# A fused attention and spectral-mixing kernel: a fixed order of weight loads, x times w_ch moved behind the attention, and two spreads held back until the last weights have landed

## The chip, the core and the metric

The kernel runs on one core of a Trainium2 chip. The metric is the device time of one execution in microseconds (us). Three timed runs of the kernel before gave 440.73, 440.25 and 440.62 us; their median is 440.62. The profiled execution took 440.91 us as a whole, and its span, from the first to the last instruction that the profile shows, is 439.1 us.

Engines are named as in the profile: PE multiplies matrices (PEld loads its stationary operand), DVE and ACT are the vector and scalar engines, POOL issues the large loads from DRAM, SP issues the small transfers and the output.

## What is computed

Attention over 8 batches and 8 heads (576 positions, head size 64) with a causal mask and a decay bias, and then, on its output x (8 x 576 x 512), a mixing in the frequency domain and a residual block:

```python
scores = scale * q @ k.T ; scores = where(causal, -1e9, scores + minimum(-(cum_i - cum_j), 0))
x = softmax(scores) @ v                      # heads side by side: 8 x 576 x 512
X = rfft(x, axis=1)                          # only the first 64 modes are used
Yr = einsum('bmd,mde->bme', Xr, w_r) - einsum('bmd,mde->bme', Xi, w_i)
Yi = einsum('bmd,mde->bme', Xr, w_i) + einsum('bmd,mde->bme', Xi, w_r)
y = irfft(Yr + 1j * Yi, n=576, axis=1)       # zero beyond mode 64
u = x + y
out = u + maximum(u @ w_ch, 0)
```

w_r and w_i are 64 x 512 x 512 each in float32: 134 MB that are read once. Everything else is small beside them.

## The kernel before

**Groups, chunks, tiles.** The 512 columns of x are cut into 4 groups of 128 (two heads each), the 64 modes into 8 chunks of 8. A weight tile is one group, one chunk, and one of w_r and w_i: 64 tiles, numbered 0 to 63 in the order of use, each 1 MB on chip (bf16), loaded by two DMAs of 512 KB. Chunk product c (0 to 31, `modes`, L470) uses tiles 2c and 2c+1: sixteen matmuls, the first eight on the w_r tile, the other eight on the w_i tile. Groups 0 to 2 (chunks 0 to 23) add into `y_acc`; group 3 (chunks 24 to 31) adds the last part and gives the spectrum `yb` of its chunk.

**The first four tiles** lie in memory that is free early (`early`, L199). The others rotate through two rings, five tiles (`wpool`) and three (`wpool2`); `ring_of` (L209) says which. From tile 38 on only the ring of five is used, because `wpool2` then takes kept products. A tile is loaded once the tile that had its place has been used.

**The attention loop** (L591) runs over n = 0 to 31, one group and one batch per step. POOL issues, in this order by step: q and k of a later step (every second step), v, and the weight tiles up to `on_chip[n]`. `on_chip` comes from a plan (L254 to L270): up to step 7 about one tile a step, then 1.5 tiles a step, then 2, cut back where a ring has no free place. `mode_steps` says which chunk products stand in which step: chunks 0 to 3 in step 8, then one or so per step, so that all of chunks 0 to 23 are inside the loop. The transformed x of a group (`fft`, L450) goes to one of two buffers, `xs[g % 2]`.

**x times w_ch.** The output needs (x + y) @ w_ch. y @ w_ch is made chunk by chunk (`y_times_wch`), x @ w_ch is made ahead for 18 pairs of row tiles; two pairs stay in PSUM, 16 are kept on chip (`kept`). For one pair x is transposed on PE (`x_transposed`, or `first_transposed` inside the loop), multiplied by w_ch (`x_times_wch`) and copied by ACT to its place (`keep`). Six of the 16 pairs (`first_pairs`, L527) are done inside the last six steps of the loop, one in the middle of chunk 30. The other nine are done by `work()`, called between the chunk products of group 3: `TAKE = (3, 2, 3, 0, 0, 0)` calls after chunks 24, 25 and 26, and two more inside `gather` of chunk 27 (its turns 1 and 3).

**Group 3.** After each product the chunk's spectrum is transposed (`y_transposed`). The first four chunks are then turned into rows of `yv`, by `gather(0, 4)` after chunk 27: four turns, each with two sets of eight matmuls (L729) and four copies by ACT and DVE in alternation (L739, L741) that follow each other. Chunks 28 and 29 go through `y_times_wch` (L710), a DMA (`spread`, L511) and a second `gather` of their own after chunk 29, which also has three transposes of x and x @ w_ch of pair 0. Chunks 30 and 31 are spread into `yv` by DMAs on SP: `spread(6, 0)` when the spectrum of chunk 30 is made, `spread(6, 1)` when its product with w_ch is made, and both again for chunk 31. Between the quarters of chunk 31 stand `first_z` and `first_u`, the sums for pairs 0 and 1 that use chunk 30 from SBUF (`add_last`) and rows below `GK` of `yv`, so not the rows of chunks 30 and 31.

**The end.** The list of steps from L955 on makes the 18 pairs of outputs in an order written by hand, and SP writes them out. The first step that reads all 128 rows of `yv` is U1.

Of the kernel before, what the change touches and what calls it, by code (L numbers as in the profile page):

```python
# [19 lines left out]
def kernel(  # L20
# [11 lines left out]
    nc = tc.nc  # L32
# [82 lines left out]
    auxpool = aux.enter_context(tc.tile_pool(name="aux_psum", bufs=2, space=PSUM, side="right"))  # L115

    dpool = ctx.enter_context(tc.tile_pool(name="dram", bufs=1, space=bass.MemoryType.DRAM))
    ncum_dram = dpool.tile([NPAIR, S + HP], BF16, name="ncum_dram")
    at = ExitStack()
    ap_ = at.enter_context(tc.tile_pool(name="attn", bufs=1))  # L120
# [125 lines left out]


    NW = 2
    mode_steps = {B: [0, 1, 2, 3], B + 1: [4], B + 2: [5], B + 4: [6], B + 6: [7]}
    for c in range(NCK, (NG - 1) * NCK):  # L250
        mode_steps.setdefault(B + c - (0 < c % NCK < 4), []).append(c)
    used = [NW * sum(len(cs) for t, cs in mode_steps.items() if t < n) for n in range(N + 1)]
    W0 = 2
    on_chip = []  # L254
    for n in range(N):
        w = 4 + 2 * (WA + WB + NE - 2) * (n + 1) // (B + 1) if n < B else plan + (3 if n <= 2 * B else 4)
        plan = w

        nt, ring = 0, ([], [])
        while nt < min(w // 2, len(wq)):  # L260
            i = ring_of(nt)
            if i is not None:
                depth = (WA, WB)[i]
                if len(ring[i]) >= depth and ring[i][-depth] >= used[n]:
                    break
                ring[i].append(nt)
            nt += 1
        if nt < w // 2:
            plan = 2 * nt + 1
        on_chip.append(2 * nt)  # L270


    nc.sync.dma_start(out=s_sb, in_=s.rearrange("b h t -> (b h) t"))
# [176 lines left out]
    def fft(n):  # L450
        if n < 0:
            return
        g, b = divmod(n, B)
        ps = auxpool.tile([P, 2, 3 * HM], FP32, name="ft_ps", tag="aux")
        for T in range(NT):
            nT = tails[T]
            for q_ in range(2):
                nc.tensor.matmul(  # L458
                    ps[HP * q_ : HP * q_ + HP].rearrange("p h f -> p (h f)"),
                    x_all[:nT, g, b, T, q_::2], Ff_sb[:nT, T, :],  # L460
                    start=(T == 0), stop=(T == NT - 1),
                    tile_position=(0, HP * q_), skip_group_check=True,
                )
        for h in range(2):
            for q_ in range(2):
                a = ps[HP * q_ : HP * q_ + HP, h, : 2 * HM].rearrange("p (r m) -> p r m", r=2)
                a = bass.AP(tensor=a.tensor, offset=a.offset, ap=[a.ap[0], [HM, 2]] + list(a.ap[1:]))
                nc.vector.tensor_copy(out=xs[g % 2][HP * h : HP * h + HP, q_, :, h, :, b, :], in_=a)  # L468

    def modes(g, c, meanwhile=None):  # L470


        ps = auxpool.tile([P, DM], FP32, name="yp", tag="aux")
        cols = xs[g % 2].rearrange("p q k h r b m -> p q k (h r b) m")

        def product(ri, q_, cg):
            k0 = HP if ri == 1 and c == 0 and cg == 0 else 0
            nc.tensor.matmul(  # L478
                ps[32 * cg : 32 * cg + 32, :],
                cols[k0:, q_, 1 - ri, :, c * MC // 2 + cg],  # L480
                wt[(g, c, ri)][cg // 2][k0:, 2 * (cg % 2) + q_, :],
                start=(ri == 0 and q_ == 0), stop=(ri == 1 and q_ == 1),
                tile_position=(k0, 32 * cg), skip_group_check=True,
            )

        for x in range(4):
            ri, y = divmod(x, 2)
            if meanwhile and x in meanwhile:
                meanwhile[x]()
            for z in range(4):  # L490
                if meanwhile:
                    product(ri, z // 2, 2 * y + z % 2)
                else:
                    product(ri, y, z)
        if g == 0:
            nc.vector.tensor_copy(out=y_acc[:, c, :], in_=ps)
# [27 lines left out]

    ways = dict(zip(kept, "vsgmsgsgmsgsgsgs"))

    first_pairs = [i for i in kept[1:] if pairs[i][0][1] < NF and pairs[i][0][0] <= 4][:6]  # L527
    z1s, xts1 = {}, {}

    def kept_place(i, t):  # L530

# [12 lines left out]
    def first_transposed(i, x):  # L544
        b, T = pairs[i][x]
        ps = auxpool.tile([P, DT, P], FP32, name="xt_ps", tag="aux")
        for dt in range(DT):
            nc.tensor.matmul(
                ps[:, dt, :], x_all[:, dt, b, T, :], ident16h, start=True, stop=True,
                skip_group_check=True,  # L550
            )
        xts1[i, x] = spool.tile([P, DT, P], FP16, name="xt1", tag="yt")
        nc.vector.tensor_copy(out=xts1[i, x], in_=ps)

    open_unit = {}

    def half_of(pool, name):
# [8 lines left out]
    def first_product(i, x):  # L566
        if x == 0:
            kept_place(i, half_of(wpool2, "z1"))
        ps = auxpool.tile([P, DM], FP32, name="z1_ps", tag="aux")
        for dt in range(DT):  # L570
            nc.tensor.matmul(
                ps, xts1[i, x][:, dt, :], wch_sb[:, dt, :], start=(dt == 0), stop=(dt == DT - 1)
            )
        keep_product(i, x, ps)


    def mode_products(n, half=None):
        cs = mode_steps.get(n, [])
# [3 lines left out]
    with tc.tile_pool(name="sc_psum", bufs=2, space=PSUM) as scpool, \  # L582
# [6 lines left out]
        load(loads_qk(2) + loads_v(2))  # L589
        pad_p()  # L590
        for n in range(N):  # L591
            if n in (0, 2):
# [17 lines left out]
            mode_products(n)  # L610
            transposes(n + 1, 0)
            scores(n, 1)
            i = first_pairs[n - N + len(first_pairs)] if n >= N - len(first_pairs) else None
# [8 lines left out]
            if i is not None:  # L622
                first_product(i, 1)
        av(N - 1, 1)
        fft(N - 1)
    load(loads_w(2 * len(wq)))
# [16 lines left out]
    NLOC = 5  # L643
    old = xs_flat[0]
# [6 lines left out]
    places = [finpool.tile([P, 4 * DM], BF16, name="r_sb", tag="r", bufs=3) for i in range(2)]  # L651
    places += [finpool.tile([P, 4 * DM], BF16, name=f"z1_{i}") for i in range(NLOC)]
    places.append(old[:, 4 * DM : 8 * DM])
# [33 lines left out]
    def keep(i):  # L687
        x_times_wch(i, True)
        j = late.index(i)
        kept_place(i, places[j])  # L690
        for x in range(2):
            keep_product(i, x, zs.pop((i, x)))

# [13 lines left out]
    def y_times_wch(c, yt):  # L707
        vp = auxpool.tile([P, DM], FP32, name="v_ps", tag="aux")
        for dt in range(DT):
            nc.tensor.matmul(  # L710
                vp, yt[:, dt, :], wch_sb[:, dt, :], start=(dt == 0), stop=(dt == DT - 1)
            )
# [171 lines left out]
    yb6 = modes(NG - 1, c, {2: lambda: keep(late[-1])})  # L884
# [114 lines left out]
```

## Time and profile before

| what | value |
|---|---|
| median of three runs | 440.62 us |
| profiled execution, as a whole | 440.91 us |
| its span | 439.1 us |
| PE, DVE, ACT, POOL busy | 344.2, 252.3, 226.0, 171.4 us |
| mean granted PE clock | 0.909 |
| loads by POOL (queue q0) | 61424 packets, 81.28 MB |
| transfers by SP (queue q1) | 6936 packets, 11.14 MB |
| HBM read, written | 163.37 MB, 9.51 MB |
| longest wait of POOL for PE | 13.28 us, ended at 382.85 us |

The times in the profile count from the start of the span. The 40 slices of the page are 11 us each. A line of the timeline gives start, duration, engine, source line, operation, operands, shape and count, and in brackets how long the engine had been idle and what ended that. A line of a table by windows gives the length, the busy time and count for each engine, the granted clock of PE as a share of full speed, the busy share of the DMA engines (over 1 where packets of an engine overlap) and the rate in GB/s of what was written.

### The profile page before, as it was taken

Reading aid. Unit: us, or ns where it says so; the run is one execution under the profiler, and the core shown is the slowest. Engines: PE = TensorE matmul, PEld = TensorE weight load, DVE = VectorE, ACT = ScalarE, POOL = GpSimd, SP = SyncE. Lnnn points to the kernel's source line nnn. Section 1 sums busy time; section 2 is a strip of 40 time slices with the busy share of each in tenths; the row PEclk is TensorE's granted clock in tenths of the full one; section 3 lists DMA queues with packets and bytes.
Section 4 is the critical chain, followed back from the end, with each engine's and each line's share of the span. In section 5 each row is a group of like instructions: output and inputs, shape, how many; then the busy total and the mean of one; then the engine's idle time right before and its main releaser. Section 6 shows DMA issues by size and latency. Waiting matters only on the chain.

```text
span 439.1 us, 10583 instructions
## 1 busy us (share of the span) xinstructions
PE 344.2 (78%) x4409; PEld 205.8 (47%) x4409; DVE 252.3 (57%) x574; ACT 226.0 (51%) x421; POOL 171.4 (39%) x257
## 2 busy tenths in 40 slices
PE   1598899899695977983938548889996986769994
PEld 1365566466463534651615225555653544433441
DVE  7667776677564545672624325666655542462795
ACT  1386888268563724760725124566661442422794
POOL 6555444344354443423434334433322221130293
PEclk9998999999987969895877866999997996999999
DMA  8999999999999999999999999999999999997498
GB/s 162 207 205 207 204 206 208 207 209 207 208 206 206 209 207 210 208 209 209 205 209 209 209 208 207 207 209 206 212 211 212 211 211 211 201 208 154 160 381 345
DMA packets 68407, 93.09 MB, mean 212 GB/s; under 512 B 25276, under 2 KB 27064, under 8 KB 68360
## 3 DMA queue, kind: packets, MB, share of 16 engines
q0 software_dynamic: 61424, 81.28, 104.9%
q1 hardware_dynamic: 6936, 11.14, 7.0%
q8 instruction: 34, 0.56, 0.5%
q14 instruction: 13, 0.11, 0.1%
HBM read 163.37 MB, written 9.51 MB: 394 GB/s over the span
## 4 chain that ended last, share of the span: by engine, by line
DMA 52%; PE 25%; DVE 14%; issue 4%; POOL 2%; ACT 2%; DVEq 0%; POOLq 0%; ACTq 0%
DMA w_sb<-in_moe_w_r_dram 24%; DMA w_sb<-in_moe_w_i_dram 16%; DMA qk<-in_k_dram 8%; PE yp L478 3%; PE z_ps L682 3%; DMA qk<-in_q_dram 3%; DVE qt L359 3%; PE sc_ps L397 3%; DVE xs L468 2%; PE av_ps L433 2%; DVE x_all L443 2%; PE sc_ps L391 2%; PE tr_ps L355 2%; PE g_ps L729 2%; DMA v<-in_v_dram 2%
## 5 line engine op out<-in xcount | busy, mean ns | idle before, releaser
L405 ACT ACTIVATE p_sb<-sc_ps,cumt_sb 128x576 f16<-128x576 f32 (+1 forms) x256 | 141.9, 635 | 22.6 <-PE sc_ps L397 22.1
L397 PE MATMUL sc_ps<-qt,kt 128*128 128x512 bf16 (+2 forms) x384 | 78.7, 318 | 6.3 <-ACT kt L359 5.6
L244 POOL DMA_DIRECT2D v<-in_v_dram x72 | 51.3, 714 | 60.3 <-DMA w_sb<-in_moe_w_r_dram 11.6
L244 POOL DMA_DIRECT2D w_sb<-in_moe_w_i_dram x62 | 38.4, 621 | 89.7 <-PE yp L478 30.3
L359 DVE COPY qt<-tr_ps 64x576 bf16<-64x576 bf16 x64 | 47.8, 746 | 42.3 <-PE tr_ps L355 42.3
L478 PE MATMUL yp<-w_sb,xs 128*32 128x512 bf16 (+1 forms) x480 | 42.7, 434 | 26.9 <-DMA w_sb<-in_moe_w_i_dram 23.4
L355 PE MATMUL tr_ps<-ident,qk 64*64 64x64 bf16 x1152 | 34.8, 206 | 32.3 <-DMA qk<-in_k_dram 15.2
L244 POOL DMA_DIRECT2D w_sb<-in_moe_w_r_dram x60 | 37.3, 623 | 53.6 <-DMA w_sb<-in_moe_w_r_dram 32.9
L397 PEld LDWEIGHTS <-kt 128*128 128x128 bf16 x384 | 39.0, 106 | 35.0 <-ACT kt L359 12.2
L391 PE MATMUL sc_ps<-negm,ident 128*128 128x256 bf16 x256 | 54.6, 299 | 0.0
L355 PEld LDWEIGHTS <-qk 64*64 64x64 bf16 x1152 | 26.8, 119 | 50.3 <-DVE kt L359 19.5
L376 ACT ACTIVATE p<-sc_ps,cumt 128x64 f16<-128x64 f32 x32 | 10.0, 313 | 74.2 <-PE sc_ps L372 74.2
L433 PE MATMUL av_ps<-v,p_sb 128*128 128x65 f16 x1024 | 44.7, 198 | 1.9 <-DVE x_all L443 0.7
L359 ACT COPY kt<-tr_ps 64x576 bf16<-64x576 bf16 x32 | 22.8, 713 | 40.8 <-DVE qt L359 40.1
L433 PEld LDWEIGHTS <-p_sb 128*128 128x128 f16 x1024 | 38.0, 100 | 9.8 <-DVE x_all L443 5.6
L468 DVE CAST xs<-ft_ps 64x128 bf16<-64x128 f32 x128 | 36.7, 287 | 6.9 <-PE ft_ps L458 5.5
L438 DVE TENSOR_REDUCE den<-av_ps 128x5 f32<-128x10 f32 x64 | 10.8, 169 | 49.9 <-PE av_ps L433 48.9
L478 PEld LDWEIGHTS <-xs 128*32 128x32 bf16 (+1 forms) x512 | 17.4, 145 | 44.7 <-DMA w_sb<-in_moe_w_i_dram 26.0
L443 DVE TENSOR_TENSOR x_all<-av_ps,rcp 128x320 f16<-128x320 f32 x64 | 31.5, 491 | 2.2
L498 DVE TENSOR_TENSOR y_acc<-yp,y_acc 128x512 f32<-128x512 f32 x16 | 11.1, 691 | 28.8 <-PE yp L478 28.0
L458 PE MATMUL ft_ps<-Ff_sb,x_all 128*64 128x192 f16 (+1 forms) x320 | 24.2, 264 | 1.0 <-DVE x_all L443 1.0
L359 DVE COPY kt<-tr_ps 64x576 bf16<-64x576 bf16 x32 | 24.4, 763 | 0.4
(110 smaller groups left out, 429.5 us busy)
## 6 DMA issues: line engine op xcount, KB each, us to landing
w_sb<-in_moe_w_r_dram POOLq DMA_DIRECT2D x60, 512.0 KB, 13.5
w_sb<-in_moe_w_i_dram POOLq DMA_DIRECT2D x55, 512.0 KB, 13.2
out_dram<-r_w SPq DMA_DIRECT2D x16, 512.0 KB
v<-in_v_dram POOLq DMA_DIRECT2D x72, 64.0 KB, 11.1
qk<-in_q_dram POOLq DMA_DIRECT2D x15, 288.0 KB, 11.9
qk<-in_k_dram POOLq DMA_DIRECT2D x15, 288.0 KB, 13.2
x_all<-in_moe_w_r_dram POOLq DMA_DIRECT2D x4, 512.0 KB, 8.8
w_sb<-in_moe_w_i_dram POOLq DMA_DIRECT2D x3, 384.0 KB, 12.7
```

Of the source, the lines that this page charges most:

```text
L244: nc.gpsimd.dma_start(out=dst, in_=src)
L355: nc.tensor.transpose(ps[rows, r, :], src[rows, r, :], ident16[rows, rows])
L359: copy(out=to[:, :, :, half * RH : half * RH + RH], in_=ps[HP * i : HP * i + HP].rearrange("d r (h p) -> d h p r", h=2),)
L391: nc.tensor.matmul(ps[:, bass.ds(w * S, W)], ident16, negm[:, bass.ts(r, W)], start=True, stop=False, skip_group_check=True,)
L397: nc.tensor.matmul(ps[:, c0 : c0 + i1 - i0], keys[:, w, r, :], qh[:, i0:i1], start=False, stop=True, skip_group_check=True,)
L405: nc.scalar.activation(out=pt[:, poff[x] : poff[x] + S - w * W], in_=ps[:, w * S : (w + 1) * S - w * W], func=ACTF.Exp, bias=cumt_sb[:, x, ...
L433: nc.tensor.matmul(ps[:, I, r : r + NCH], lhsT, rhs, start=(i == 0), stop=(i == len(todo) - 1), skip_group_check=True,)
L443: nc.vector.tensor_tensor(out=x_all[:, g, b, :, D * h : D * h + D], in0=ps[:, :, 1 : NCH], in1=rcp.unsqueeze(2).to_broadcast([P, NT, D]), ...
L458: nc.tensor.matmul(ps[HP * q_ : HP * q_ + HP].rearrange("p h f -> p (h f)"), x_all[:nT, g, b, T, q_::2], Ff_sb[:nT, T, :], start=(T == 0), ...
L468: nc.vector.tensor_copy(out=xs[g % 2][HP * h : HP * h + HP, q_, :, h, :, b, :], in_=a)
L478: nc.tensor.matmul(ps[32 * cg : 32 * cg + 32, :], cols[k0:, q_, 1 - ri, :, c * MC // 2 + cg], wt[(g, c, ri)][cg // 2][k0:, 2 * (cg % 2) + ...
L682: nc.tensor.matmul(zs[i, x], xts[i][:, x, dt, :], wch_sb[:, dt, :], start=(dt == 0), stop=(last and dt == DT - 1), skip_group_check=True,)
```

## The change

- **Weights and attention.** The plan is replaced by a fixed rule: `3 + n` tiles by step n below 8, then `4 + n + (n - 8) // 8`, so one tile a step and one more every eight steps; an assertion checks the places in the rings. `mode_steps` is written out: chunks 0 to 16 stand in steps 8 to 30, and chunks 17 to 23 come after the loop. A third buffer `xs` lets group 3 be transformed while group 2 is still to be used (`XS = (0, 1, 2, 0)`).
- **x times w_ch.** `first_pairs`, `first_transposed` and `first_product` go. All 15 pairs but the last are done by `work()` after the loop: three calls after each of chunks 18 to 21, one after 22, two after 23, one after 25. None is left after chunks 24 and 26 and inside `gather` of chunk 27. The places of the kept products change accordingly.
- **Spreads.** `spread(6, 0)` and `spread(6, 1)` are no longer issued where their data are made. Ahead of chunk 31 SP is given a DMA of four bytes (`mark`) that reads the last bytes of the last weight tile, and so waits for their landing, and then the two spreads.

```diff
-    xs = [gp.tile([P, 2, 2, 2, 2, B, HM], BF16, name=f"xs{i}") for i in range(2)]
+    xs = [gp.tile([P, 2, 2, 2, 2, B, HM], BF16, name=f"xs{i}") for i in range(3)]
+    XS = (0, 1, 2, 0)
...
-    mode_steps = {B: [0, 1, 2, 3], B + 1: [4], B + 2: [5], B + 4: [6], B + 6: [7]}
-    for c in range(NCK, (NG - 1) * NCK):
-        mode_steps.setdefault(B + c - (0 < c % NCK < 4), []).append(c)
+    mode_steps = {
+        B: [0, 1, 2, 3], 9: [4], 10: [5], 12: [6], 14: [7], 16: [8], 18: [9], 19: [10], 21: [11], 23: [12],
+        25: [13], 26: [14], 28: [15], 30: [16],
+    }
+    done = [c for t in sorted(mode_steps) for c in mode_steps[t]]
...
-        w = 4 + 2 * (WA + WB + NE - 2) * (n + 1) // (B + 1) if n < B else plan + (3 if n <= 2 * B else 4)
-        plan = w
...
+        w = 3 + n if n < B else 4 + n + (n - B) // B
+        for u in range(NE, w):
+            ring = [x for x in range(NE, u + 1) if ring_of(x) == ring_of(u)]
+            depth = (WA, WB)[ring_of(u)]
+            assert len(ring) <= depth or ring[-1 - depth] < used[n], (n, u)
+        on_chip.append(2 * w)
...
-            if c >= NCK - 2:
+            if c >= NCK - 1:
                 spread(c, 0, yb)
...
-            if i is not None:
-                first_transposed(i, 0)
             transposes(n + 1, 1)
             fft(n - 1)
             av(n, 0)
-            if i is not None:
-                first_product(i, 0)
-                first_transposed(i, 1)
-            if i is not None:
-                first_product(i, 1)
...
-        spread(c, 1, vb)
+        if c < NCK - 2:
+            spread(c, 1, vb)
...
-    late = [i for i in kept if i not in first_pairs]
+    late = list(kept)
+    assert len(places) == len(late)
     order_z = late[:-1]
-    TAKE = (3, 2, 3, 0, 0, 0)
+    TAKE = {18: 3, 19: 3, 20: 3, 21: 3, 22: 1, 23: 2, 25: 1}
...
+    for c in range(len(done), (NG - 1) * NCK):
+        modes(c // NCK, c % NCK)
+        for x in range(TAKE.get(c, 0)):
+            work()
     for c in range(NCK - 2):
         yb = modes(NG - 1, c)
-        for x in range(TAKE[c] - 1):
-            work()
...
-        if TAKE[c]:
+        for x in range(TAKE.get((NG - 1) * NCK + c, 0)):
             work()
...
-            gather(0, NY, (1, 3), (1, 0))
+            gather(0, NY, (), (1, 0))
...
+    nc.sync.dma_start(
+        out=mark[:1], in_=wt[(NG - 1, NCK - 1, 1)][1][HP : HP + 1, WM - 1, :2]
+    )
+    spread(c, 0, yb6)
+    spread(c, 1, vb6)
```

More of the change, by code (lines that the diff above doesn't have):

```diff
@@ L117 @@
     dpool = ctx.enter_context(tc.tile_pool(name="dram", bufs=1, space=bass.MemoryType.DRAM))
+    mark = dpool.tile([1, 2], BF16, name="mark")
     ncum_dram = dpool.tile([NPAIR, S + HP], BF16, name="ncum_dram")
@@ L255 @@
     for n in range(N):
-        w = 4 + 2 * (WA + WB + NE - 2) * (n + 1) // (B + 1) if n < B else plan + (3 if n <= 2 * B else 4)
-        plan = w
-        nt, ring = 0, ([], [])
-        while nt < min(w // 2, len(wq)):
-            i = ring_of(nt)
-            if i is not None:
[L263 to L270, printed above, removed]
+        w = 3 + n if n < B else 4 + n + (n - B) // B
[4 more added lines that the diff above has]
+        on_chip.append(2 * w)
     nc.sync.dma_start(out=s_sb, in_=s.rearrange("b h t -> (b h) t"))
@@ L467, in fft @@
                 a = bass.AP(tensor=a.tensor, offset=a.offset, ap=[a.ap[0], [HM, 2]] + list(a.ap[1:]))
-                nc.vector.tensor_copy(out=xs[g % 2][HP * h : HP * h + HP, q_, :, h, :, b, :], in_=a)
+                nc.vector.tensor_copy(out=xs[XS[g]][HP * h : HP * h + HP, q_, :, h, :, b, :], in_=a)
     def modes(g, c, meanwhile=None):
         ps = auxpool.tile([P, DM], FP32, name="yp", tag="aux")
-        cols = xs[g % 2].rearrange("p q k h r b m -> p q k (h r b) m")
+        cols = xs[XS[g]].rearrange("p q k h r b m -> p q k (h r b) m")
         def product(ri, q_, cg):
@@ L525 @@
     ways = dict(zip(kept, "vsgmsgsgmsgsgsgs"))
-    first_pairs = [i for i in kept[1:] if pairs[i][0][1] < NF and pairs[i][0][0] <= 4][:6]
-    z1s, xts1 = {}, {}
+    z1s = {}
     def kept_place(i, t):
@@ L542, in keep_product @@
         nc.vector.tensor_tensor(out=z1s[i][:, 1, xx], in0=z, in1=z1s[i][:, 0, xx], op=ALU.subtract)
[L544 to L553, printed above, removed]
     open_unit = {}
@@ L564, in half_of @@
         return t[:, :HU]
[L566 to L574, printed above, removed]
     def mode_products(n, half=None):
@@ L591 @@
         for n in range(N):
-            if n in (0, 2):
+            if n in (0, 2, 4):
                 nc.vector.memset(xs_flat[n // 2].bitcast(FP32), 0.0)
@@ L612 @@
             scores(n, 1)
-            i = first_pairs[n - N + len(first_pairs)] if n >= N - len(first_pairs) else None
-            if i is not None:
-                first_transposed(i, 0)
             transposes(n + 1, 1)
@@ L618 @@
             av(n, 0)
-            if i is not None:
-                first_product(i, 0)
-                first_transposed(i, 1)
-            if i is not None:
-                first_product(i, 1)
         av(N - 1, 1)
@@ L641 @@
     upool = xt.enter_context(tc.tile_pool(name="u_psum", bufs=2, space=PSUM))
-    NLOC = 5
-    old = xs_flat[0]
+    NLOC = 3
+    old = xs_flat[1]
     xt_sb = [
@@ L649 @@
     xt_sb.append(finpool.tile([P, 2, DT, P], FP16, name="xt_x"))
-    places = [finpool.tile([P, 4 * DM], BF16, name="r_sb", tag="r", bufs=3) for i in range(2)]
+    places = [lambda: half_of(wpool2, "z1")] * (2 * WB)
+    places.append(old[:, 4 * DM : 8 * DM])
+    places += [finpool.tile([P, 4 * DM], BF16, name="r_sb", tag="r", bufs=3) for i in range(2)]
     places += [finpool.tile([P, 4 * DM], BF16, name=f"z1_{i}") for i in range(NLOC)]
-    places.append(old[:, 4 * DM : 8 * DM])
+    places += [xs_flat[2][:, i * 4 * DM : (i + 1) * 4 * DM] for i in range(2)]
     places += [y_acc[:, c : c + 2, :].rearrange("p c e -> p (c e)").bitcast(BF16) for c in (0, 2)]
@@ L689, in keep @@
         j = late.index(i)
-        kept_place(i, places[j])
+        kept_place(i, places[j]() if callable(places[j]) else places[j])
         for x in range(2):
```

## The prediction

> **What bounds the kernel now.** I read the page first: the rate of the transfers over the 40 slices.
>
> ```profile
> span 439.1 us, 10583 instructions
> ...
> GB/s 162 207 205 207 204 206 208 207 209 207 208 206 206 209 207 210 208 209 209 205 209 209 209 208 207 207 209 206 212 211 212 211 211 211 201 208 154 160 381 345
> ```
>
> From the second slice to the 36th the rate stands at 201 to 212, whatever the engines do: 204 to 210 while q, k and v come too, 211 when only weights are left. The first 400 us are the weight stream; work moved about under it is free as long as the stream is fed and PE is on time at its end. So next comes the end, in the chain of waits:
>
> ```profile
> 42.65 0.49 DVE x_all L443
> ...
> 49.28 0.49 DVE x_all L443
> ...
> 347.38 16.27 DMA w_sb<-in_moe_w_i_dram
> 363.69 0.69 PE yp L478 x7
> ...
> 384.54 1.05 PE yp L478 x15
> ...
> 394.72 0.67 PE yp L478 x8
> ...
> 405.29 0.60 PE yp L478 x4
> ```
>
> The last link that is a transfer ends at 363.6 (chunk 27). From there the chain is PE with DVE and ACT: chunk 29 at 384.5, 30 at 394.7, the last quarter of 31 at 405.3. PE is late by its own work, though by little: the last weight DMA is issued at 388.85 and lands 16.0 us later, at 404.9. Stream and PE end within half a microsecond of each other; a gain needs both, a loss only one. (The first two lines show one early step of attention: 6.63 us.)
>
> Third, PE's clock, by the windows (length, busy time and count for PE, PEld, DVE, ACT, POOL, then clock, DMA share, GB/s):
>
> ```profile
> 366.01:369.42 3.41, 2.42 (x16) 1.56 (x17) 0.57 (x1) 1.21 (x3) 1.07 (x2) 0.50 1.12 211
> 369.42:372.83 3.41, 3.23 (x25) 2.77 (x25) 1.33 (x3) 1.06 (x2) 0.15 (x1) 0.50 1.12 211
> 382.00:384.00 2.00, 0.90 (x7) 0.49 (x8) 0.31 (x1) 0.58 (x1) 1.15 (x2) 1.00 0.86 161
> 384.00:386.00 2.00, 2.00 (x27) 1.06 (x26) 1.08 (x2) 0.00 (x0) 1.85 (x4) 1.00 1.06 172
> 393.31:396.72 3.41, 2.00 (x15) 0.91 (x16) 2.10 (x4) 2.04 (x4) 0.00 (x0) 1.00 1.12 213
> ```
>
> The clock changes in steps of 3.41 us. In the first window PE is 71% busy at half clock and stays there; in the second, 95% busy, it is released, and stays at 1.00 to the end. What made the second window full was the `work()` inside `gather` (371.95 to 374.6). In the last one 59% is enough to stay released. The timeline prices half clock:
>
> ```profile
> 226.55 1.09 PE L478 MATMUL yp<-w_sb,xs 128*32 128x512 bf16 x8 [4.08 <-DMA w_sb<-in_moe_w_i_dram]
> 341.06 1.33 PE L682 MATMUL z_ps<-wch_sb,xs 128*128 128x512 f16 x3
> 366.22 1.99 PE L729 MATMUL g_ps<-wch_sb,yt_first 128*64 128x512 f16 x8 [0.68 <-ACT yt_first L704]
> 369.60 1.98 PE L729 MATMUL g_ps<-wch_sb,yt_first 128*64 128x512 f16 x8 [0.95 <-DVE yv L739]
> 377.17 1.14 PE L729 MATMUL g_ps<-wch_sb,yt_first 128*64 128x512 f16 x8 [0.99 <-DVE yv L739]
> 380.48 1.09 PE L478 MATMUL yp<-w_sb,xs 128*32 128x512 bf16 x16
> 383.50 1.04 PE L710 MATMUL v_ps<-wch_sb,yt_first 128*128 128x512 f16 x4 [0.73 <-ACT yt_first L704]
> ```
>
> A chunk's eight matmuls take 1.09 us cold where sixteen take 1.09 warm; three 512-wide ones take 1.33, so four about 1.8, against 1.04 warm. A turn of `gather` lasts 3.38 cold (366.22 to 369.60) and 2.54 warm (374.63 to 377.17).
>
> **Attention at its own pace.** Each step brings 0.43 MB of q, k, v (issues of 288 KB for q and k every second step, twice 64 KB of v), and the change gives it one tile (1.05 MB) and every eighth step one more: 1.61 MB, at 207 GB/s 7.8 us. A step computes in 6.63; a chunk product adds about 1 (1.09 of PE, 0.69 of DVE), and 13 chunks fall on the last 23 steps: 7.2. The loads stay slower than the steps, so the stream stays fed. All bytes are the same, and steps 0 to 9 load as before. Gain 0; if the cover goes, a step of 8.3 would starve the stream by 0.5 for 22 steps, 11 us. After the loop three `work()` calls take 7.2 us before (338.6 to 345.8), with a chunk 8.3, under the 9.9 that two tiles take: free as well, and removing `first_pairs` saves nothing for the same reason. The third buffer adds one memset of 1.8 us on DVE (the row at 32.83) in step 4, under the stream.
>
> **Gather without work, at half clock.** In the new order PE has, after chunk 23, only one `work()` (after 25): some 2 us of 10 around chunk 26, so it comes to chunk 27 at half clock. Before it did too (0.50 from 366.01). Now nothing fills a window. Each turn keeps PE busy 2.42 of 3.38, 72%, the share that did not release it above. So: the late half of chunk 27 at 363.69 as before, +0.4 (1.09 for 0.66) and +0.2 (its transposes, where eight take 1.03 cold and 0.62 warm) puts the first turn at 366.8; four turns of 3.38 end at 380.4. Before, with two works and two warm turns, chunk 28 began at 380.48. The works leave and the clock takes their room.
>
> Chunk 28 then runs cold. Before, 3.99 us from its start to that of chunk 29 (380.48 to 384.47). Now +1.0 (sixteen matmuls at 2 x 1.09 overlapped, about 2.05), +0.2 (transposes), +0.8 (`v_ps`): 6.0, so chunk 29 starts at 386.4 against 384.47, +1.9. Its sixteen matmuls, cold, +1.0: +2.9. From `v_ps` on PE is busy without a break, so the window up to about 390 is full and releases it before the 1.9 us product of pair 0; the transposes of x wait for DVE anyway. Nothing later has slack: chunk 30 waited for the second gather's copies, and from there to 405.2 PE is busy without a gap. So +2.9 reaches the end. Bounds: +1.8, if the clock is released ahead of chunk 29's product and 28's `v_ps`; +4.6, if the wait before chunk 30 (59% busy above) now falls below what holds the clock and costs one window of half clock, 1.7 us.
>
> A rule bears on this. The Trainium skill, "TensorE: Matmul & The Clock Gate" (Part 1: The HAM clock gate), says that about 3.4 us of sustained activity release the clock and an idle window takes it back. Taken plainly the gather would be released after one turn, the others would take 2.54, chunk 28 would start at 366.8 + 3.4 + 7.6 = 377.8 and nothing would be late. By the row above, 71% busy did not release it, and I go by the row.
>
> **The stream's end.** POOL's 13.28 us wait ended at 382.85, and the rate fell to 161 and 172 for 4 us: (50 + 39) x 2 / 211 = 0.8 us lost. It waits for chunk 28, which starts when it did, half a microsecond slower: between 0 and 1.3 lost, gain 0. The two spreads (128 KB each) leave the stream: at most 2 x 0.62 = 1.2 us at 211 GB/s, at least 0 if they only fill gaps; I take 0.6. With PE late by 2.9, the stream at about 404.3 no longer sets the end, and this gain is hidden.
>
> **The new wait on SP.** Behind `mark` stand the four spreads and the output. Three issues of 0.55 us from 404.9 are over at 406.6; before, `spread(7, 0)` was issued at 406.70, and now its data come at 409.6. The first to read all rows is U1 (410.26, now 413). Cost 0; without that cover up to 1.7.
>
> **Sum.** 0 + 2.9 + 0 = 2.9 us on the profiled execution (span 439.1, 440.91 as a whole, 0.29 above the median). On the median: 440.6 + 2.9 = 443.5.
>
> **Rivals.** (A) *Faster: PE stays or becomes released in chunks 27 to 28.* For it: the gate's windows run free of the program, and before it was released at 372.83. Then the shorter gather lets chunk 28 start by 378, and chunk 29 when its tile is there (issued 363.93, 19.6 us to landing: 383.5, and 0.4 of issue), half a microsecond earlier than now; half of POOL's hole closes (0.4 of 0.8) and the spreads give 0.6: -1.0, 439.6. It decides on one point, whether chunk 29 starts before 384.5. Against it: 72% busy. (B) *Everything hidden*: the stream is a little better, PE a little late, 440.6 +- 0.8; it needs chunk 29 within 0.9 us of now. (C) *The stream starves in the loop* because the steps, with v and q buffers of fixed depth, don't keep up: +3 to +11, 444 to 452; against it the 207 GB/s at 6.63 us a step early on.
>
> **Numbers.** Forecast 0.53, A 0.25, B 0.14, C 0.08. The likeliest: 443.5, with its own range 442.3 to 445.3. The range for 8 in 10 has to take A in at the lower side: 439.3 to 445.5. A measurement can tell about 0.2% from no change (0.9 us): faster 0.26, the same 0.14, slower 0.60.
>
> **What would show it.** Right: clock 0.50 in the windows from 366 to about 390, four gather turns of 3.4, chunk 29's product at 386 or later, chunk 31's last quarter near 408, the stream over by 405 and the output shifted as a whole. Wrong: turns of 2.5 us, chunk 29 at 384; or rates under 200 GB/s before 270 us (C); or U1 waiting for a spread.

## The result, and the profile after

Four runs of the changed kernel gave 443.63, 444.94, 445.15 and 445.50 us, median 445.04; four of the kernel before beside them 440.24 to 440.73, median 440.44. The ratio is 1.0099, 95% interval 1.0075 to 1.0123: slower by 4.6 us. The profiled execution is the fastest of the four (443.63 us, span 441.9), 2.7 us above the profiled execution before. The page shows the stream:

```profile
span 441.9 us, 10614 instructions
...
GB/s 160 208 205 205 206 206 209 206 209 207 204 206 207 208 208 209 203 205 209 208 208 208 199 212 212 210 211 211 211 211 211 211 211 211 211 215 96 149 382 350
```

From the second slice to the 36th the rate stands at 199 to 215, and from the 24th on at 210 or more; the dip to 201 that the 35th slice of the kernel before has, where POOL waited, is gone. The last packet of a weight ends at 403.58, before at 404.62. The stream gained a microsecond, and the kernel lost. The windows of the end are next, cut where the granted clock can change (length, busy time and count for PE, PEld, DVE, ACT, POOL, then clock, DMA share, GB/s):

```profile
364.78:368.19 3.41, 2.60 (x18) 1.55 (x17) 0.00 (x0) 1.13 (x3) 0.61 (x1) 0.50 1.12 211
368.19:371.61 3.42, 2.42 (x16) 1.90 (x16) 1.30 (x2) 1.10 (x4) 0.61 (x1) 0.50 1.12 211
371.61:375.02 3.41, 2.43 (x16) 1.90 (x16) 1.30 (x3) 1.09 (x3) 0.00 (x0) 0.50 1.13 211
375.02:378.43 3.41, 2.42 (x16) 2.01 (x16) 1.33 (x3) 1.10 (x3) 0.00 (x0) 0.50 1.12 211
381.85:385.26 3.41, 2.66 (x12) 0.98 (x16) 0.13 (x1) 0.59 (x1) 1.14 (x2) 0.50 1.12 211
385.26:388.67 3.41, 2.98 (x28) 1.54 (x21) 2.22 (x4) 0.00 (x0) 2.25 (x4) 0.50 1.12 211
388.67:392.08 3.41, 3.23 (x36) 1.75 (x34) 1.66 (x4) 0.59 (x1) 0.13 (x1) 1.00 1.12 222
```

PE is 71 to 76% busy in each window of the gather and stays at half clock; the window from 381.85, 78% busy, does not release it either. The one that ends at 388.67 is 87% busy, and from there the clock is 1.00. Before, it was released at 372.83. PE's timeline gives what that costs:

```profile
362.47 1.08 PE L473 MATMUL yp<-w_sb,xs 128*32 128x512 bf16 x8 [3.77 <-DMA w_sb<-in_moe_w_i_dram]
365.63 1.98 PE L696 MATMUL g_ps<-wch_sb,yt_first 128*64 128x512 f16 x8 [0.68 <-ACT yt_first L670]
369.01 1.98 PE L696 MATMUL g_ps<-wch_sb,yt_first 128*64 128x512 f16 x8 [0.96 <-DVE yv L706]
...
379.14 1.93 PE L473 MATMUL yp<-w_sb,xs 128*32 128x512 bf16 x16 [0.95 <-DVE yv L706]
383.20 1.89 PE L676 MATMUL v_ps<-wch_sb,yt_first 128*128 128x512 f16 x4 [0.73 <-ACT yt_first L670]
385.02 1.94 PE L473 MATMUL yp<-w_sb,xs 128*32 128x512 bf16 x16
396.23 0.66 PE L473 MATMUL yp<-w_sb,xs 128*32 128x512 bf16 x8 [1.88 <-DVE yv L706]
406.73 0.65 PE L473 MATMUL yp<-w_sb,xs 128*32 128x512 bf16 x4
413.10 0.62 PE L742 MATMUL u_ps<-yv,G_sb 128*64 128x512 f16 x4 [1.26 <-DMA yv<-y_sb]
```

The same places in the kernel before (the late half of chunk 27, the last quarter of chunk 31, U1):

```profile
363.69 0.66 PE L478 MATMUL yp<-w_sb,xs 128*32 128x512 bf16 x8 [2.07 <-DMA w_sb<-in_moe_w_i_dram]
405.22 0.65 PE L478 MATMUL yp<-w_sb,xs 128*32 128x512 bf16 x4
410.26 0.62 PE L774 MATMUL u_ps<-yv,G_sb 128*64 128x512 f16 x4
```

The turns of the changed kernel are 3.38 us each. From the late half of chunk 27 (362.47) to the last quarter of chunk 31 (406.73) PE takes 44.26 us; before 41.53 (363.69 to 405.22). That is 2.73 more, of which 1.22 is hidden, since the last tile of chunk 27 landed that much earlier. U1, the last line of the changed kernel, has a wait that it did not have before. The chain of waits says for what:

```profile
407.76 0.42 DVE y_sb L497
408.19 0.02 issue
408.20 4.85 DMA yv<-y_sb
413.05 0.04 issue
413.10 0.62 PE u_ps L742 x4
```

`spread(7, 0)` was issued 0.02 us after its data were made, so `mark` does not hold it up. The trace marks the landing of each of its 16 shares: 15 come within 2.87 us, the last after 4.85. At 410.08, in its flight, stands one packet of 16 KB of the queue that the page lists as "q8 instruction". The profiled execution's 2.7 us are thus 1.5 of PE's half clock and 1.26 of this wait.

### The profile page after: what moved, and what is told of

It reads as the page before. It is cut to its first block, busy times and chain, and to the rows that moved or that the text cites. A ratio compares the mean times of both kernels' runs of the same rounds, so it can differ in the third digit from the quotient of the medians.

```text
span 441.9 us, 10614 instructions
## 1 busy us (share of the span) xinstructions
PE 344.4 (78%) x4409; PEld 202.1 (46%) x4409; DVE 253.6 (57%) x575; ACT 226.0 (51%) x421; POOL 171.3 (39%) x257
## 4 chain that ended last, share of the span: by engine, by line
DMA 59%; PE 19%; DVE 14%; issue 3%; ACT 3%; POOL 1%; DVEq 0%; POOLq 0%; ACTq 0%
DMA w_sb<-in_moe_w_i_dram 30%; DMA w_sb<-in_moe_w_r_dram 17%; DMA qk<-in_q_dram 7%; PE yp L473 3%; DVE qt L354 3%; DMA qk<-in_k_dram 2%; DVE xs L463 2%; PE g_ps L696 2%; PE av_ps L428 2%; PE sc_ps L392 2%; DVE x_all L438 2%; PE tr_ps L350 2%; DVE kt L354 2%; PE z_ps L742 2%; DMA v<-in_v_dram 2%
## 5 line engine op out<-in xcount | busy, mean ns | idle before, releaser
L392 PE MATMUL sc_ps<-qt,kt 128*128 128x512 bf16 (+2 forms) x384 | 73.9, 303 | 8.0 <-ACT kt L354 5.8
L473 PE MATMUL yp<-w_sb,xs 128*32 128x512 bf16 (+1 forms) x480 | 45.8, 460 | 37.9 <-DMA w_sb<-in_moe_w_i_dram 27.9
L392 PEld LDWEIGHTS <-kt 128*128 128x128 bf16 x384 | 36.3, 101 | 35.6 <-ACT kt L354 16.0
L386 PE MATMUL sc_ps<-negm,ident 128*128 128x256 bf16 x256 | 51.8, 286 | 0.2
L350 PE MATMUL tr_ps<-ident,qk 64*64 64x64 bf16 x1152 | 31.8, 200 | 21.8 <-DVE kt L354 19.3
L428 PE MATMUL av_ps<-v,p_sb 128*128 128x65 f16 x1024 | 43.6, 196 | 3.5 <-issue 1.6
L428 PEld LDWEIGHTS <-p_sb 128*128 128x128 f16 x1024 | 36.4, 99 | 11.8 <-DVE x_all L438 5.9
L350 PEld LDWEIGHTS <-qk 64*64 64x64 bf16 x1152 | 24.5, 113 | 35.4 <-DVE kt L354 25.8
L497 DVE TENSOR_TENSOR y_sb<-yp,y_acc 128x512 f16<-128x512 f32 (+1 forms) x9 | 5.6, 631 | 40.0 <-PE yp L473 40.0
L533 ACT COPY z<-z_ps 128x512 f32<-128x512 f32 x18 | 10.5, 586 | 29.6 <-PE z_ps L648 16.5
```

The source lines that it names most:

```text
L350: nc.tensor.transpose(ps[rows, r, :], src[rows, r, :], ident16[rows, rows])
L386: nc.tensor.matmul(ps[:, bass.ds(w * S, W)], ident16, negm[:, bass.ts(r, W)], start=True, stop=False, skip_group_check=True,)
L392: nc.tensor.matmul(ps[:, c0 : c0 + i1 - i0], keys[:, w, r, :], qh[:, i0:i1], start=False, stop=True, skip_group_check=True,)
L428: nc.tensor.matmul(ps[:, I, r : r + NCH], lhsT, rhs, start=(i == 0), stop=(i == len(todo) - 1), skip_group_check=True,)
L473: nc.tensor.matmul(ps[32 * cg : 32 * cg + 32, :], cols[k0:, q_, 1 - ri, :, c * MC // 2 + cg], wt[(g, c, ri)][cg // 2][k0:, 2 * (cg % 2) + ...
```

## Experiments

Each ratio is against the kernel before on the same chip (medians 440.31, 440.62 and 440.38 on the three chips used). "Before" and "after" name the two kernels. Idle products are matmuls into a PSUM tile that nothing reads; they change nothing of the output. Cold and warm mean a granted clock of 0.50 and of 1.00; the output stage is the time from the start of U1 to the end.

### 1. Two works back in the gather

```diff
-    TAKE = {18: 3, 19: 3, 20: 3, 21: 3, 22: 1, 23: 2, 25: 1}
+    TAKE = {18: 3, 19: 3, 20: 3, 21: 3, 22: 1, 23: 1}
...
-            gather(0, NY, (), (1, 0))
+            gather(0, NY, (1, 3), (1, 0))
```

> The changed kernel (445.0 us median, 443.6 in its profiled run, where chunk 28 starts at 379.1, chunk 30 at 396.2 and the last quarter of chunk 31 at 406.7) with two of the work calls put back into the gather of chunk 27: one fewer after chunk 23 and none after 25. Theory (clock): PE is at half clock from chunk 26 on and the bare gather never fills a window, so chunks 28 and 29 run cold and the end comes later. Then the works release the clock in the gather as they did before; chunk 28 starts no earlier (380 to 381) but warm, chunk 30 at 394.5 to 395, and the time is 440.4 to 442, 3 to 4.5 us less. Rival (spreads): the loss is in the late spreads that the first sum over all rows of yv waits for; then this run stays at 443.5 to 445.5. Rival (loads): the loss is in the attention loop's order; then it stays too.

441.93 us (440.60 to 442.78, 7 runs), ratio 1.0035 [1.0021, 1.0048], 3.1 us less than the changed kernel. Its windows:

```profile
368.34:371.75 3.41, 3.08 (x24) 2.61 (x23) 1.33 (x3) 1.09 (x3) 0.61 (x1) 0.50 1.12 210
371.75:375.16 3.41, 3.41 (x27) 2.20 (x26) 2.14 (x4) 1.52 (x4) 0.00 (x0) 1.00 1.12 212
```

The first work makes one window 90% busy, the clock is released at 371.75, chunk 29 starts at 383.47, the last quarter of chunk 31 at 404.22, 2.5 us before that of the changed kernel. More work in the gather, and less time: most of the loss is the clock's. U1 still waits 1.46 us on `yv` in this profile, so not all of the loss comes back.

### 2. The spreads as before

```diff
-            if c >= NCK - 1:
+            if c >= NCK - 2:
                 spread(c, 0, yb)
...
-        if c < NCK - 2:
-            spread(c, 1, vb)
+        spread(c, 1, vb)
...
-    nc.sync.dma_start(
-        out=mark[:1], in_=wt[(NG - 1, NCK - 1, 1)][1][HP : HP + 1, WM - 1, :2]
-    )
-    spread(c, 0, yb6)
-    spread(c, 1, vb6)
```

> The changed kernel with the two spreads of chunk 30 issued where their data are made, without the marking transfer. Rival (spreads): the late spreads cost the 1.26 us that U1 waited in the profiled run, and more in the other runs: 440.5 to 443. Theory (clock): the wait of U1 was a chance meeting with another transfer, and the spreads cost or bring nothing that shows, since PE is late: 444 to 446, chunk 30 again at 396 and cold matmuls in chunks 28 and 29.

444.47 us (442.85 to 445.86, 6 runs), ratio 1.0088 [1.0068, 1.0109]: within the noise the same as with the third part of the change. U1 waits 0.80 us without `mark` too: again one landing mark of `spread(7, 0)` is late (4.39 us), with a code packet in its flight (410.83). The profile shows a further loss of the clock that the other profile of the same gather did not have:

```profile
393.56:396.97 3.41, 1.28 (x25) 0.66 (x25) 2.27 (x4) 1.75 (x4) 0.00 (x0) 1.00 1.11 208
396.97:400.38 3.41, 3.41 (x12) 1.14 (x14) 0.69 (x1) 1.21 (x3) 0.00 (x0) 0.50 1.04 207
```

The wait ahead of chunk 30 falls into one window, which is 37% busy, and the next is served at half clock: the 1.90 us product in it takes 3.42, and the last quarter comes at 408.27.

### 3. PE kept busy ahead of the gather

```diff
+        if c == NY - 1:
+            idle_matmuls(6)
+        fill = {NY - 1: 7, NCK - 3: 9}.get(c)
-        yb = modes(NG - 1, c)
+        yb = modes(NG - 1, c, fill and {2: lambda: idle_matmuls(fill)})
```

> The changed kernel with matmuls that nothing reads, in PE's waits alone: six ahead of chunk 27, seven between the halves of chunk 27 and nine between those of chunk 29, 512 columns each into a scratch bank. No work is moved, so this touches the clock alone. Theory (clock): released during chunk 27, gather turns of 2.5 instead of 3.4 us, chunk 28 at 375 to 377, chunk 29's late half at 383 to 384 as its tile lands, chunk 30 at 393 to 394; then the stream (404) sets the end: 439.5 to 441.5. Rivals (spreads, loads): more work on PE and nothing gained, 444.5 to 446.

447.70 us (443.33 to 448.52, 6 runs), ratio 1.0154 [1.0123, 1.0185]. A miss, and an instructive one:

```profile
360.78:364.19 3.41, 1.06 (x12) 0.43 (x12) 0.69 (x1) 0.00 (x0) 0.75 (x2) 1.00 1.12 210
364.19:367.60 3.41, 2.42 (x16) 1.56 (x17) 0.13 (x1) 1.33 (x3) 0.61 (x1) 0.50 1.12 212
```

The idle products did release the clock, and at full clock they were over in half the time, so that the wait for the tile (2.62 us) left a window 31% busy and the gather began cold again. The nine in chunk 29 ran cold and stood in the way with 3.49 us. A longer output stage (30.55 us, see experiment 6) adds to the miss.

### 4. The kernel before with a bare gather

```diff
-    TAKE = (3, 2, 3, 0, 0, 0)
+    TAKE = (4, 3, 3, 0, 0, 0)
...
-            gather(0, NY, (1, 3), (1, 0))
+            gather(0, NY, (), (1, 0))
```

> The kernel before with only the two works taken out of the gather of chunk 27: one more after chunk 24 and one more after chunk 25. Loads, loop and spreads are those of before. Theory (clock): PE is idle in chunk 27 and the bare gather runs all four turns at 3.4 us, chunks 28 and 29 run cold: 442 to 445, 1.5 to 4.5 us over the kernel before. Rivals (spreads, loads): this has neither of the causes and stays at 440.0 to 441, or is faster because POOL's wait of 13 us gets shorter.

441.15 us (440.04 to 442.20, 12 runs), ratio 1.0017 [1.0006, 1.0029]. The expected 442 to 445 did not come:

```profile
364.83:368.25 3.42, 2.30 (x23) 2.20 (x25) 1.30 (x2) 1.13 (x3) 1.22 (x2) 1.00 1.12 211
368.25:371.66 3.41, 2.35 (x28) 2.08 (x25) 1.30 (x2) 1.51 (x3) 0.00 (x0) 1.00 1.13 212
371.66:375.07 3.41, 1.55 (x16) 1.54 (x16) 2.01 (x4) 1.67 (x4) 0.00 (x0) 1.00 1.12 211
375.07:378.48 3.41, 2.55 (x20) 1.02 (x19) 1.28 (x2) 0.00 (x0) 0.60 (x1) 0.50 1.12 211
```

Here the works end at 362, PE comes into the gather at full clock, and with 67 to 69% busy it stays there; the turns are 2.54. It is lost only after a window with 45%, and chunks 28 and 29 still run cold: the last quarter comes at 406.20, 1.0 us later than before, in a profiled execution that is one of the slowest of the twelve (442.15). So the bare gather alone is not what costs: it costs when PE arrives cold, which the change's order (one work in the last 25 us ahead of it) sees to. 68% holds the clock, 72% does not bring it back.

### 5. Idle products inside the gather

```diff
+            if fill and (c0 == 0 or b0 + ng >= B):
+                idle_matmuls(fill)
             if b0 // ng in turns:
                 work()
...
-            gather(0, NY, (), (1, 0))
+            gather(0, NY, (), (1, 0), 2)
```

> The changed kernel with two matmuls that nothing reads at the end of each of the four turns of the gather of chunk 27, where PE waits 0.95 us for DVE's copies: 0.86 us of PE at half clock, so a turn at half clock is 97% busy in place of 72% and no longer for it. Nothing else is touched. Theory (clock): the window of a turn now releases the clock, at the latest in the second turn; turns of 3.4, 3.4, 2.5, 2.5, chunk 28 at 376 to 378 and warm, chunk 29's late half when its tile lands (383 to 384), chunk 30 near 393.5: 440.5 to 442.5, some 3 us under the changed kernel. If the loss lies elsewhere, nothing is gained: 444 to 446.

442.05 us (441.26 to 442.84, 12 runs), ratio 1.0027 [1.0014, 1.0040]. PE's timeline:

```profile
367.94 1.03 PE L688 MATMUL idle_ps<-wch_sb,ident16h 128*128 128x512 f16 x2
368.96 1.98 PE L701 MATMUL g_ps<-wch_sb,yt_first 128*64 128x512 f16 x8
372.34 1.14 PE L701 MATMUL g_ps<-wch_sb,yt_first 128*64 128x512 f16 x8 [0.20 <-DVE yv L711]
377.40 1.09 PE L473 MATMUL yp<-w_sb,xs 128*32 128x512 bf16 x16 [0.44 <-DVE yv L711]
```

Two products that nothing reads fill the waits of a turn; the clock is released at 371.78, and 3.0 us come back, as with the works. Only products in PE's waits were added, and the last quarter of chunk 31 comes at 404.26, 2.47 us earlier: that settles the clock. (Ahead of chunk 30 it is lost once even here, after a window 34% busy.) But two other things changed with it. U1 (409.30) no longer waits, and it starts 0.96 earlier than in the kernel before; yet the end comes 0.36 us later, because the output stage takes 30.20 us, before 28.88.

### 6. Filling the other waits

Three variants: four more idle products in chunk 29 and five at the end of the second gather (first); the latter alone in the kernel before (second) and in that of experiment 1 (third).

```diff
-        yb = modes(NG - 1, c)
+        yb = modes(NG - 1, c, {2: lambda: idle_matmuls(4)} if c == NCK - 3 else None)
...
-                gather(NY, NCK - 2, (), (0,))
+                gather(NY, NCK - 2, (), (0,), 5)
```

> The same, with four such matmuls between the halves of chunk 29 and five at the end of the second gather, ahead of chunk 30, where PE waits 1.9 us (a window there was 37% busy and cost a second stretch of half clock in one profile, 55 to 59% in others). Theory (clock): no stretch of half clock is left from chunk 28 to the end, and the runs spread less: 439.5 to 441.5, at or under the run with the gather alone filled. If the second wait doesn't matter, the same time as that run.

> The kernel before with five such matmuls at the end of its second gather alone, where its window was 59% busy in the profile. Theory (clock): some of its runs lose the clock there, and these are gained: 439.5 to 440.3 at the median, at most 0.2% under the kernel before, with less spread. If that wait never costs it the clock, the same time to 0.1%.

> The changed kernel with two works back in the gather (441.9 in its own run, 440.6 to 442.8, where U1 waited 1.46 us for a spread) and five such matmuls at the end of the second gather. Theory (clock): the runs that lost the clock ahead of chunk 30 are gained: 440.5 to 441.5, about 0.5 to 1 less. What is then left over the kernel before is the wait of U1 for the spread of chunk 31 (0.8 to 1.5 in the profiles), in which a transfer of code stands on one engine before one sixteenth of the spread; the further matmuls shift that transfer, and where it no longer meets the spread U1 does not wait and the time is 439 to 440.

441.77 (ratio 1.0028 [1.0016, 1.0040]), 441.08 (1.0006 [0.9990, 1.0021]) and 442.79 us (1.0046 [1.0030, 1.0062]). In the first the clock stays at 1.00 from 371.60 to 436.45, the last quarter starts at 403.86 (1.36 earlier than before), and the time still lies 1.2 us above the kernel before. The third is slower than experiment 1, although U1 no longer waits. In the first and third the output stage takes 30.22 and 30.39 us, in the second 28.89.

The packets of the instruction queue explain this, as far as the profiles go. They come once for 256 instructions of PE (matmuls and weight loads together: 34 packets for the 8818 here), each 16 KB, 0.9 to 1.7 us long. Adding products moves them. The Trainium skill, "Runtime: NRT & Kernel Launch" (Instruction fetch mechanics), says the same of the block, 16 KiB or 256 instructions, and that the cost of crossing one is mostly hidden. What a packet does to other transfers is another matter. The last packets of each profile, and what stood beside them:

| kernel | packets (us) | share of spread(7, 0) that lands last | U1 waits | U1 to end |
|---|---|---|---|---|
| before | 392.3, 408.4 | 3.02 | 0 | 28.88 |
| after | 393.8, 410.1 | 4.85 (15 by 2.87) | 1.26 | 28.77 |
| experiment 1 | 391.5, 407.1, 440.8 | 5.05 (15 by 3.58) | 1.46 | 28.77 |
| experiment 2 | 393.8, 410.8, 444.7 | 4.39 | 0.80 | 28.84 |
| experiment 4 | 390.5, 409.5 | 2.98 | 0 | 28.90 |
| experiment 5 | 389.2, 404.8, 430.0 | 3.50 | 0 | 30.20 |
| 6, first | 389.2, 402.6, 429.3 | 4.21 (all late) | 0.80 | 30.22 |
| 6, second | 392.4, 408.2 | 3.59 (15 by 2.87) | 0 | 28.89 |
| 6, third | 392.7, 404.9, 431.3 | 3.21 | 0 | 30.39 |
| experiment 3 | 394.3, 407.9, 434.1 | 2.90 | 0 | 30.55 |

In all four profiles with a packet between 429 and 435 us the output stage is 1.3 to 1.7 us longer; in all others it takes 28.77 to 29.31. The landing marks of the output transfers show how. In experiment 5, the transfer that SP issued at 427.53 has its last share 0.14 us behind the 15th; the one issued at 428.80, whose flight holds the packet of 430.04, has it 1.54 behind, and each of the five after it 1.41 to 1.50, up to the end. The other three kernels show the same, by 1.4 to 1.9 us; in the kernel before no share is more than 0.23 behind in that stretch. So one of the 16 shares falls behind at the packet and never catches up. There SP issues the transfers 0.6 to 1.7 us apart while each takes some 3 us to land, which is probably why.

With the spread it is less regular: one share is late in the changed kernel and in experiments 1, 2 and 6 (second), but in the kernel before a packet stands in its flight too (408.4, the spread from 406.70 to 409.72) and delays nothing, and so it is in experiment 4. The trace does not name the DMA engine of a packet, so whether it must meet the engine that still has its share to move was not shown. Experiment 7 moves the packets out of both places.

### 7. The code packets moved

```diff
+    def code(n):
+        ps = upool.tile([P, DM], FP32, name="idle_ps", tag="u")
+        for j in range(n):
+            nc.tensor.matmul(ps[:HP, :HP], ident16h[:HP, :HP], ident16h[:HP, :HP], start=True, stop=True, skip_group_check=True)
+
+    extra = {(NG - 2, NCK - 1): 46, (NG - 1, 1): 45}
...
+            if x == 2 and (g, c) in extra:
+                code(extra[g, c])
```

> The kernel after the change with 91 small idle products (64*64, each with its weight load) in PE's idle time between the tiles of chunks 23 and 25, 320 to 343 us. They compute nothing that is read; they shift the places at which a block of 256 PE instructions ends, so that the packet of PE's code that met spread(7,0) at 410.1 us comes some 70 to 80 instructions later, 3 to 6 us behind the first yv product of the output stage. Theory of the code packet: that product no longer waits 1.26 us on yv, and the time falls by 0.8 to 1.3 from 445.0, to 443.7 to 444.2. Rival, that spread (7,0) is late for the other spreads beside it: the wait stays and the time is 445.0 within 0.4. The clock's part is the same in both: the gather's four turns stay at 0.50 with 3.38 us each.

> The gather filled with two idle products a turn (442.05), and 75 small idle products between the tiles of chunks 23 and 25, which shift PE's code packets so that none comes in the last 20 us of the output. Theory of the code packet: from the first yv product to the end 28.8 us instead of 30.2, and the time falls by 1.2 to 1.5, to 440.6 to 440.9. Rival, that the later end came of the idle products themselves or of an earlier output: the 30.2 us stay, and the time is 442.0 within 0.4.

The changed kernel with 91 small products early: 443.80 us (441.88 to 445.12, 8 runs), ratio 1.0065 [1.0041, 1.0089]. The kernel of experiment 5 with 75: 441.11 us (440.47 to 442.52, 12 runs), ratio 1.0012 [0.9998, 1.0025]. U1 in the two profiles:

```profile
413.89 0.62 PE L751 MATMUL u_ps<-yv,G_sb 128*64 128x512 f16 x4
```

```profile
409.86 0.62 PE L758 MATMUL u_ps<-yv,G_sb 128*64 128x512 f16 x4 [0.75 <-DMA yv<-y_sb]
```

In the first the packet comes at 416.58, all shares of `spread(7, 0)` land within 2.90 us, and U1 does not wait. In the second the packet comes at 413.95 instead of 404.78 and 430.04, and the output stage takes 29.07 us instead of 30.20: one share of the output transfer issued at 412.91 is 1.97 us late, but so early in the output the lag shrinks, to 0.3 at the end. Both readings hold: a code packet in the flight of `spread(7, 0)` can cost U1 0.8 to 1.5 us, and one some ten to twelve microseconds before the end of the output, where the lag stays, 1.3 to 1.7. In time the two are 1.2 and 0.9 us better than without the shift (the second a little less than expected), but the intervals of the ratios overlap: shown by the profiles, only likely by the times.

The 0.75 us wait of the second is another thing, as is the 0.80 of the first of experiment 6: no packet is near, but all shares are late (the last 4.19 us), because the two held-back spreads were issued 1.3 and 0.6 us ahead of this one. The mark, then, does cost something once PE is no longer late: without it (experiment 8, first) there is no such wait.

### 8. Early spreads in the filled kernel, and the third part of the change alone

The first is the first of experiment 6 with the edit of experiment 2 and 67 small products; the second is the kernel before with `mark` and the late spreads, the edit of experiment 2 the other way round.

```diff
+    extra = {(NG - 2, NCK - 1): 34, (NG - 1, 1): 33}
...
-            if c >= NCK - 1:
+            if c >= NCK - 2:
                 spread(c, 0, yb)
```

```diff
-            if c >= NCK - 2:
+            if c >= NCK - 1:
                 spread(c, 0, yb)
...
+    spread(c, 0, yb6)
+    spread(c, 1, vb6)
```

> All of PE's waits filled (441.77), without the mark and with chunk 30's spreads where its data are made, as in the kernel before, and 67 small idle products that shift PE's code packets as in the run beside it. If clock, late spreads and code packet together are what the change loses, the time is 441.77 - 1.36 (the end 28.8 us behind the first yv product) - 0.80 (that product's wait) = 439.6, some 0.8 below the kernel before. If the spreads of chunk 30 under the last weights hold these up, as the change supposes, chunk 31's last quarter comes 0.5 to 1 us later than 403.9 and the time is 440.1 to 440.6. If the code packets are no cause it is 441 to 441.8.

> The kernel before with the third part of the change alone: the mark, and chunk 30's spreads behind it. The last weights land 0.5 to 1 us earlier than 404.62, but PE's own chain sets the last quarter of chunk 31 (405.22), so nothing comes of it: 440.2 to 440.7. If the weights' last landing sets the end, as the change supposes: 439.4 to 439.9. If the late spreads hold up spread(7,0): 441 to 441.7.

440.87 us (440.27 to 441.41, 12 runs), ratio 1.0005 [0.9990, 1.0020], and 440.34 us (439.83 to 442.63, 12 runs), ratio 0.9998 [0.9983, 1.0014]. In the first U1 does not wait; its time is 0.9 us better, not the 2.2 expected: the last quarter comes 0.5 later (404.40, the spreads again beside the last weights) and the output stage takes 29.31 (a packet at 413.67). In the second the last packet of a weight ends at 403.31 and the last quarter starts at 403.64, 1.6 us earlier than in the profile of the kernel before. That is not the spreads' doing alone: with the same program up to chunk 30, PE here came into the gather warm, and chunk 28 began at 376.58 instead of 380.48. Then

```profile
409.51 0.62 PE L776 MATMUL u_ps<-yv,G_sb 128*64 128x512 f16 x4 [0.77 <-DMA yv<-y_sb]
```

U1 gives half of it back, as in experiment 7, to the three spreads that now leave together (the span is 438.3), and in the median nothing is left. The third part of the change alone is worth nothing that can be measured. No version beats the kernel before.

## Why the prediction was right, and where its sizes were off

The forecast of 443.5 us and "slower" rested on one mechanism, and that one was at work; rivals A (PE released) and B (hidden) fell.

- *Gather at half clock.* Right in mechanism and size: turns of 3.38 us, half clock to 388.67 where "about 390" stood, 5.88 us from chunk 28 to 29 where 6.0 stood, PE's way from chunk 27 to the last quarter of chunk 31 2.73 us longer where 2.9 stood. ("Before it did too" holds for the gather alone: before, PE came to chunk 27 warm and lost the clock at 366.01.) Experiments 1 and 5 show it: with the gather's waits filled, and loads and spreads as in the changed kernel, the last quarter comes 2.5 us earlier and the time falls by 3.
- *"The late half of chunk 27 at 363.69 as before".* This step was off. It came at 362.47, so that only 1.5 of the 2.73 us reached the last quarter: 406.73, not "near 408", and chunk 29's product came at 385.02, not at "386 or later". Why the tile landed 1.2 us earlier was not settled.
- *The upper bound with one more cold window, 1.7 us.* Not chosen, but it is met: in the profiles of experiments 2 and 7 (first) the last quarter starts at 408.27 and 408.85. It comes where one window happens to hold the whole wait ahead of chunk 30: in experiment 2 the window 393.56 to 396.97 holds all of it (394.3 to 396.2), in the changed kernel's profile a border at 395.50 divides it. The changed kernel's other three runs, 1.3 to 1.9 us above the profiled one with mean clocks of 0.885 to 0.894 against 0.905, fit that; they have no trace, so for them this is inferred and not shown.
- *"Cost 0" for U1's wait.* Wrong by 1.26 us, and U1 waiting for a spread was one of the prediction's own signs of being wrong. It came not through `mark`: experiment 2 has the wait without it. The prediction priced SP's queue and did not see that the moved program also moves PE's code packets. It is a term missing from the sum: 1.5 + 1.26 make up the profiled 2.7, and the forecast's 2.9 was near it by luck, because two errors cancelled. The median's 4.6 is above both, probably by the second cold window.
- *The stream.* Last weights 1.04 us earlier where 0.6 was taken (bounds 0 to 1.2): hidden, as said. Experiment 8 (second) finds no gain from it in the median without the other two parts either. Rival C did not occur, although one slice before 270 us stands at 199 GB/s, just under the 200 that was named as its sign: none is lower, and the last weights came early.
- *The rule.* The Trainium skill's "TensorE: Matmul & The Clock Gate" (Part 1: The HAM clock gate) has PE released after a busy window of about 3.4 us and throttled after an idle one. The 3.41 us grid agrees with these windows. What is "busy" had to come from the row, and going by the row was right: 71 to 78% did not count. Nor need a window be idle to lose the clock: here 31 to 45% busy lost it.

## What to carry to other kernels

Before work is moved out of a stretch where PE waits in short steps, ask in which clock state PE enters it: moved work takes its activity with it, and the stretch may lose in clock what it gains in length. To fill such waits with idle products costs little if they lie inside the short waits of the loop (experiment 5); ahead of a long wait for a transfer they did not help (experiment 3). And where two ends are level to half a microsecond, a change of a few instructions moves the code packets too, so check in the profile what they meet before a difference of one microsecond is explained otherwise.

## What the runs showed of the hardware that was not expected

- The clock has a memory between its two levels: 67 to 69% busy held 1.00 (experiment 4), 71 to 78% did not release it (the changed kernel), nor did 82% (the first turn of experiment 5). From 360 to 400 us in all profiles, windows of 87% and more released the clock, windows of 49% and more held it, and windows of 31 to 45% lost it. The share alone is no full rule: in the kernel before the window from 335.29, 99% busy in the profile, left the clock at 0.50, and the next, 87% busy, released it.
- Activity at full clock lasts half as long: the seven idle products of experiment 3 took 1.68 us and could not hold the clock that six others at half clock (2.77 us) had won.
- PE's code packets, 16 KB for 256 instructions, are not free where transfers are on the path: one of the 16 shares of a transfer can fall behind by 0.7 to 2.2 us. That cost 0.8 to 1.5 us ahead of U1 and 1.3 to 1.7 at the end of the output; early in the output the lag shrinks to 0.3 to 0.5. Whether the packets under the weight stream cost anything was not measured.
